# Linear attention and a hard-swish MLP on one core: the leftover tokens' x turned by a crossbar DMA, and w_in's first pieces gated earlier

## The chip, the core and the metric

The kernel runs on one core of a Trainium2 chip. The core has a TensorE for matmuls (PE in the profile, PEld for its weight loads), a VectorE (DVE), a ScalarE (ACT), a GpSimd (POOL) and a SyncE (SP). DMAs are issued by SP, ACT or POOL, each in the order of its own instruction stream, and move data through the core's 16 DMA engines. The metric is the device time of one execution in microseconds; lower is better. The kernel before took 325.93 us (median of three runs, 325.25 to 325.99).

## What is computed

```python
def _attn_ref(q, k, v, omega):               # q, k, v: (8 batches, 8 heads, 576 tokens, 64), f32
    q_s, k_s = q * scale, k * scale          # scale = 64 ** -0.25
    def phi(x):                              # omega: (128 features, 64)
        h = einsum('bhsd,md->bhsm', x, omega) - sum(x * x, -1) / 2
        return exp(h - max(h, -1)) / sqrt(m)
    q_p, k_p = phi(q_s), phi(k_s)
    kv = einsum('bhsm,bhsd->bhmd', k_p, v)
    z = sum(k_p, axis=2)
    num = einsum('bhsm,bhmd->bhsd', q_p, kv)
    den = einsum('bhsm,bhm->bhs', q_p, z)[..., None] + 1e-06
    return num / den

def _moe_ref(x, w_in, w_out):                # x: (4608, 512), w_in: (512, 2048), w_out: (2048, 512)
    h = x @ w_in
    return (h * clip(h + 3, 0, 6) / 6) @ w_out
```

x is the attention's result with the heads of one token side by side. Each batch has 576 tokens: 512 that the kernel calls main, and 64 leftovers.

## The kernel before

**Blocks.** The MLP runs in nine blocks of 512 tokens. Blocks 0 to 7 are the main tokens of batches 0 to 7; block 8 collects the leftovers of all eight batches. Of each block, mm1 (L826; in two halves of 256 tokens for block 0, L854) multiplies x by w_in in 16 steps of four matmuls each, ACT and DVE form the activation gT, and mm2 (L885) multiplies gT by w_out in 4 chunks of 128 tokens. A chunk has four quarters of four matmuls; quarter g needs piece g of w_out. The result goes through osb (four buffers, filled by ACT or DVE) and an out DMA that SP issues.

**Attention of one batch** (L538). k and q are turned so that the head dimension lies on the partitions: kT and qT. The PE does this for batches 0 and 1 (the groups Tk and Tq, L422); from batch 2 on SP issues crossbar transposes (Tdmak and Tdmaq, L622). K (L632) multiplies kT by omega, ACT takes the exponential, and DVE reduces a maximum per row, whose reciprocal scales the rows of v (vc, L737, on POOL or DVE). Q (L649) does the same for q without the maximum. For each of four pairs of heads m, kv (L750, L752) sums over the tokens, num (L773) multiplies by the queries' features, in two parts A and B, and div (L789, DVE) divides and writes x in token order into xb. A pair's part B holds the last main group (i = 3) and the leftovers (i = 4).

**x for the MLP.** xb has two buffers, for even and odd batches: 128 partitions by 4 pairs by 640 columns, that is five groups of 128 per pair, the fifth one being the leftovers. The main groups are turned into xT, by the PE for batches 0 and 1 (X), by one crossbar transpose per pair from batch 2 on (Xdma, L818). The leftovers are turned into xS, for every batch, by e_S (L684): four 64-column matmuls against the identity matrix, here called S.0 to S.7, and a copy from PSUM by DVE or ACT (Sev). mm1 of block 8 reads xS.

**Weights and loads.** w_in comes in four pieces and w_out in four (L467, L474), and from batch 1 on also k and q: POOL issues these DMAs, because they cast f32 to bf16. v and the first batch go over SP. Each load has a gate: a key in the list of reads, whose writer must have finished. `W_GATE` (L335) names the gates of the four w_in pieces: v's landing. Batch 1's k waits for w_in's piece 2 and its q for piece 3 (L927), w_out for the landing of batch 1's q (L928), batch 2's k and q for w_out's pieces 2 and 3.

**What sets the order.** Every operation is recorded by `op` with the engines that may do it, its cost, its priority and its dependencies. A planner (`schedule`, L103) then runs a model of all engines and DMA queues and fixes which engine does what and in which order; each engine gets one stream in that order, with semaphore waits where a dependency crosses engines. For a DMA the model uses `occ`, the time in its queue, and `lat`, the time from there until the data may be used. Changing a number in the model can therefore change the order of every engine from that point on, and adds or removes no computation. In the first 20 us the planner fills the PE's gaps with matmuls of a constant tile (L459, idle).

In POOL's stream of before, the beginning after the identity matrix is: two casts of k, four casts of q, w_in piece 0 (wi0), vc of pair 0 (vc.0.0), wi1, wi2, wi3, vc.0.2, vc.0.3, then batch 1's k and q, and the four pieces of w_out.

Of the kernel before, what the change touches and what calls it, by code (L numbers as in the profile page):

```python
# [41 lines left out]
class Prog:  # L42
# [60 lines left out]
    def schedule(self):  # L103
# [68 lines left out]
        while len(order) < n:  # L172
# [45 lines left out]
            if o.group is not None:  # L218
                free[e] = st + o.issue
                flow(free[e], True)  # L220
                queues.setdefault(e, []).append([o, occ, free[e]])
                flow(1e9, False)
            else:
                free[e] = st + occ
                o.end = free[e]
# [89 lines left out]
def _emit(nc, es, q, k, v, omega, w_in, w_out, out):  # L315
# [19 lines left out]
    W_GATE = [("v32", 0, 1), ("v32", 0, 3), ("v32", 1, 3), ("v32", 1, 3)]  # L335
# [37 lines left out]
    xb = [sbt("xb%d" % u, [128, NJ, 640], BF16) for u in range(2)]  # L373
# [54 lines left out]
    op("SP", 0.2, lambda E: E.dma_start(om32[:], omega), -9.8, writes=["om32"], group="dom", inc=16, lat=1.8,  # L428
# [38 lines left out]
    def w_in_piece(i, gate):  # L467
        f0, f1 = WI[i]
        op("POOL", 0.72 * (f1 - f0), lambda E: E.dma_start(  # L469
            wi[:, :, 128 * f0:128 * f1], w_in[:, 128 * f0:128 * f1].rearrange("(c p) f -> p c f", p=128)),  # L470
           -8.6 + 0.05 * i, reads=gate, writes=[("wi", i)], group="dwi%d" % i, inc=16, lat=2.0, name="wi%d" % i,
           issue=0.85, packet=91.0)

    def w_out_piece(g, gate):  # L474
        op("POOL", 2.95, lambda E: E.dma_start(
            wo[:, 4 * g:4 * g + 4, :], w_out[512 * g:512 * g + 512, :].rearrange("(c p) e -> p c e", p=128)),
           -0.2 + 0.05 * g, reads=gate, writes=[("wo", g)], group="dwo%d" % g, inc=16, lat=2.0, name="wo%d" % g,
# [6 lines left out]
    def load(b, eng, gates):  # L484
# [4 lines left out]
        def dma(part, dst, src, n, keys, gate, prio, run):  # L489
# [4 lines left out]
               group="d" + part + ("c" if cast else "") + (str(pb) if b and part != "v" else ""), inc=16, lat=1.9,  # L494
# [43 lines left out]
    def attention(b):  # L538
# [80 lines left out]
        else:  # L619
            for t, cst, dst in (("k", KB[pb], kT), ("q", QB[pb], qT)):  # L620
                for i, (x0, x1) in enumerate(((0, 10), (10, 18))):
# [4 lines left out]
                       lat=1.9, name="Tdma%s.%d.%d" % (t, b, i), issue=1.2, packet=24.0)  # L626
# [55 lines left out]
        vxs = Virt(ring)  # L682

        def e_S(E):  # L684
            for j in range(NJ):
                ins = E.matmul(ring.t[vxs.slot][:, 64 * j:64 * j + 64], xb[pb][:, j, 512:640], ident[:, 0:64],
                               start=True, stop=True)
            return ins

        op("PE", 4 * 0.03, e_S, pos(11) if b else LATE, reads=[("xb", pb, j, 2) for j in range(NJ)] + ["ident"], writes=[vxs],  # L690
           alloc=[vxs], lat=0.25, slack=sl, spare=sp, name="S.%d" % b)
        op(EV_T, both(256), evac(lambda: xS[:, :, 64 * b:64 * b + 64],
                                 lambda: ring.t[vxs.slot][:, 0:256].rearrange("p (j t) -> p j t", j=NJ)),
           pos(11) if b else LATE, reads=[vxs], writes=[("xS", b)], name="Sev.%d" % b)

    def leftover(m0, m1):
# [8 lines left out]
        def e_num(E):  # L705
# [15 lines left out]
            xb[0][:, m0:m1, 512:640].rearrange("p m (a d) -> p m a d", a=2), psum()[:, :, :, 0:64],  # L721
# [3 lines left out]
    def pair(b, m, t):  # L725
# [33 lines left out]
        xv = xb[pb][:, m, :].rearrange("p (i a d) -> p a i d", a=2, d=D)  # L759

        def tail(part, i0, i1):
# [27 lines left out]
            op("DVE", dvet(128 * n), lambda E: E.tensor_tensor(xv[:, :, i0:i1, :], psum()[:, :, :, 0:64], rbc, ALU.mult),  # L789
               t + 0.01, reads=[vn, ("rec", ru)], writes=[("xb", pb, m, x) for x in part + [2] * (i1 == 5)], name="div" + nm + pt)  # L790

        def turn_x(i0, i1, part):
# [4 lines left out]
            def e_x(E):  # L797
                for i in range(i0, i1):
                    ins = turn(E, vx, b, i - i0, xb[pb][:, m, 128 * i:128 * i + 128])
# [17 lines left out]
        else:  # L817
            op("SP", 0.9, lambda E: E.dma_start_transpose(  # L818
                xT[pb][:, m, :].rearrange("p (t k) -> p t k", t=4), xb[pb][:, m, 0:512]),
               t + 0.03, reads=[("xb", pb, m, x) for x in range(2)], writes=[("xT", pb, m, x) for x in range(2)],  # L820
               group="dxT%d_%d" % (pb, m), inc=16, lat=1.9, name="Xdma" + nm, issue=1.2, packet=24.0)
# [63 lines left out]
    def mm2(blk, tc):  # L885
# [5 lines left out]
        for ci, (c0, c1) in enumerate(cols):  # L891
# [22 lines left out]
            for p0, np_, dst in dsts:  # L914
# [3 lines left out]
                   writes=[("out", blk, tc, p0, ci)], group="dout%d_%d%s" % (ou, p0, "b" if ci else ""), inc=16, lat=2.0,  # L918
                   name="out.%d.%d" % (blk, tc), packet=84.0)

    for b in range(B):
# [4 lines left out]
        elif b == 1:  # L926
            load(1, (), {"k": [("wi", 2)], "q": [("wi", 3)], "v": [("kb", 1, 16)]})  # L927
            for g, key in enumerate((("qb", 1, 16),("qb", 1, 16),("qb", 1, 16),("qb", 1, 16))):  # L928
# [68 lines left out]
```

## Time and profile before

The profile is one execution, taken by the hardware profiler.

| | |
|---|---|
| median of three runs | 325.93 us (325.25 to 325.99) |
| the profiled execution | 325.8 us, of which the span of its instructions is 324.0 us |
| PE busy | 316.0 us (98% of the span) |
| DVE, ACT, POOL busy | 209.8, 190.8, 77.9 us |
| granted TensorE clock | 0.999 of full speed |
| first matmul of mm1 | 20.37 us after the span's start |
| S groups on the PE (L686) | 32 matmuls, 33.3 to 251.7 us |
| crossbar transposes of xT (L818) | 24, from 83.1 to 249.5 us |

A line of a timeline has the start and the length in us, the engine, the source line, the operation with the tile that it writes and those that it reads, its shape, and how many such instructions follow each other; in brackets is the idle time before it and what ended that. SPq is SP's DMA issue. A line of the waits has the engine and line that waited, for whom, and the sum, the count and the longest of the waits. Matmuls are pipelined, so that one's length is more than its spacing to the next. The DMA share is the mean busy share of the 16 DMA engines; it counts overlapping transfers and can exceed 1.

### The profile page before, as it was taken

Reading aid. Unit: us, or ns where it says so; the run is one execution under the profiler, and the core shown is the slowest. Engines: PE = TensorE matmul, PEld = TensorE weight load, DVE = VectorE, ACT = ScalarE, POOL = GpSimd, SP = SyncE. Lnnn points to the kernel's source line nnn. Section 1 sums busy time; section 2 is a strip of 40 time slices with the busy share of each in tenths; the row PEclk is TensorE's granted clock in tenths of the full one; section 3 lists DMA queues with packets and bytes.
Section 4 is the critical chain, followed back from the end, with each engine's and each line's share of the span. In section 5 each row is a group of like instructions: output and inputs, shape, how many; then the busy total and the mean of one; then the engine's idle time right before and its main releaser. Section 6 shows DMA issues by size and latency. Waiting matters only on the chain.

```text
span 324.0 us, 5860 instructions
## 1 busy us (share of the span) xinstructions
PE 316.0 (98%) x2224; PEld 174.9 (54%) x2260; DVE 209.8 (65%) x464; ACT 190.8 (59%) x388; POOL 77.9 (24%) x107
## 2 busy tenths in 40 slices
PE   8999989999999999999999999999999999999996
PEld 6779755455654545555455545555555444444443
DVE  4988876498877828865776577756865354433411
ACT  3977963499585518865776477647674353444400
POOL 2825624055252402620154022402010000000000
PEclk9999999999999999999999999999999999999999
DMA  8999999999932997999479863996012201000024
GB/s 249 253 193 157 226 182 187 292 139 188 250 85 51 171 177 203 126 198 142 170 105 155 182 195 48 170 205 212 14 53 58 74 6 58 33 34 32 32 67 97
DMA packets 89516, 44.33 MB, mean 137 GB/s; under 512 B 56080, under 2 KB 85008, under 8 KB 89488
## 3 DMA queue, kind: packets, MB, share of 16 engines
q1 hardware_dynamic: 62272, 30.85, 40.1%
q0 software_dynamic: 26512, 12.46, 31.6%
q10 hardware_dynamic: 704, 0.66, 0.7%
q8 instruction: 18, 0.29, 0.4%
q14 instruction: 10, 0.08, 0.1%
HBM read 36.73 MB, written 9.44 MB: 143 GB/s over the span
## 4 chain that ended last, share of the span: by engine, by line
PE 85%; DMA 9%; POOL 2%; issue 1%; SPq 1%; DVE 0%
PE p L899 38%; PE p L841 34%; PE p L632 4%; PE p L649 4%; DMA wi<-in_moe_w_in_dram 3%; DMA wo<-in_moe_w_out_dram 3%; PE p L773 3%; DMA k<-in_q_dram 2%; PE p L750 2%; DMA q<-in_q_dram 2%; POOL k L493 1%; SPq L493 1%; PE p L752 0%; POOL wi L469 0%; POOL qb L411 0%
## 5 line engine op out<-in xcount | busy, mean ns | idle before, releaser
L899 PE MATMUL p<-wo,gT 128*128 128x512 bf16 (+2 forms) x571 | 139.7, 373 | 2.4 <-DMA wo<-in_moe_w_out_dram 1.3
L849 DVE SCALAR_TENSOR_TENSOR gT<-tsb,p 128x512 bf16<-128x512 bf16 x128 | 87.2, 684 | 58.0 <-ACT tsb L847 57.4
L847 ACT ACTIVATE tsb<-p 128x512 bf16<-128x512 f32 x128 | 77.1, 603 | 72.0 <-PE p L841 71.9
L841 PE MATMUL p<-xT,wi 128*128 128x512 bf16 x439 | 107.3, 379 | 0.5
L899 PEld LDWEIGHTS p<-wo,gT 128*128 128x128 bf16 x592 | 55.8, 98 | 56.8 <-ACT qpT L653 1.2
L841 PEld LDWEIGHTS p<-xT,wi 128*128 128x128 bf16 x448 | 42.9, 98 | 46.0 <-ACT qpT L653 0.2
L641 DVE TENSOR_REDUCE mx<-kp 128x4 f32<-128x512 bf16 x72 | 47.4, 674 | 15.9 <-ACT kp L638 15.9
L638 ACT ACTIVATE kp<-p 128x512 bf16<-128x512 f32 x72 | 41.5, 621 | 14.6 <-PE p L632 14.6
L653 ACT ACTIVATE qpT<-p 128x512 bf16<-128x512 f32 (+1 forms) x80 | 42.4, 576 | 3.4 <-PE p L649 3.3
L737 POOL TENSOR_TENSOR vc<-v,cc 128x512 bf16<-128x512 f32 x24 | 25.2, 1048 | 43.6 <-DVE cc L733 27.8
L789 DVE TENSOR_TENSOR xb<-p,rec 128x384 bf16<-128x384 f32 (+1 forms) x64 | 28.6, 476 | 0.0
L632 PE MATMUL p<-om,kT 128*128 128x256 bf16 x144 | 24.3, 273 | 0.0
L649 PE MATMUL p<-qT,om 128*128 128x512 bf16 (+1 forms) x76 | 23.2, 357 | 0.1
L410 ACT COPY osb<-p 128x512 f32<-128x512 f32 x25 | 14.8, 592 | 9.7 <-PE p L899 9.6
L411 DVE COPY osb<-p 128x512 f32<-128x512 f32 (+2 forms) x12 | 7.8, 646 | 18.2 <-PE p L899 18.1
L672 POOL TENSOR_TENSOR vcl<-vl,cc 64x260 bf16<-64x260 f32 x9 | 5.6, 622 | 54.3 <-DVE cc L668 30.9
L773 PEld LDWEIGHTS p<-kvz,qpT 128*128 128x128 bf16 x312 | 14.2, 98 | 7.3 <-DVE kvz L411 0.4
L632 PEld LDWEIGHTS p<-om,kT 128*128 128x128 bf16 x144 | 13.2, 98 | 9.0
L841 PE MATMUL p<-xS,wi 128*128 128x512 bf16 x62 | 16.2, 379 | 0.1
L493 POOL DMA_DIRECT2D k<-in_k_dram x12 | 9.2, 777 | 28.3 <-PE p L632 14.1
L866 PE MATMUL p<-xT,wi 128*128 128x256 bf16 x128 | 15.9, 273 | 0.0
L773 PE MATMUL p<-kvz,qpT 128*128 128x65 bf16 x312 | 15.6, 194 | 0.0
(70 smaller groups left out, 225.4 us busy)
## 6 DMA issues: line engine op xcount, KB each, us to landing
out_dram<-osb SPq DMA_DIRECT2D x32, 256.0 KB, 3.1
v<-in_v_dram SPq DMA_DIRECT2D x14, 512.0 KB, 5.6
wi<-in_moe_w_in_dram POOLq DMA_DIRECT2D x4, 512.0 KB, 8.1
k<-in_k_dram POOLq DMA_DIRECT2D x8, 256.0 KB, 4.6
k<-in_q_dram POOLq DMA_DIRECT2D x8, 256.0 KB, 5.7
wo<-in_moe_w_out_dram POOLq DMA_DIRECT2D x4, 512.0 KB, 9.9
kb<-in_k_dram POOLq DMA_DIRECT2D x6, 256.0 KB, 4.6
qb<-in_q_dram POOLq DMA_DIRECT2D x6, 256.0 KB, 5.7
```

Of the source, the lines that this page charges most:

```text
L632: ins = E.matmul(ring.t[vK.slot][:, 256 * i:256 * i + 256], kT[:, 2 * u + i, :], om[:].rearrange("d t m -> d (t m)"), start=True, stop=True)
L638: op("ACT", actt(512), lambda E, u=u, vK=vK: E.activation(kp[pb][:, 4 * u:4 * u + 4, :].rearrange("p c m -> p (c m)"), ring.t[vK.slot], AF ...
L641: op("DVE", dvet(512), lambda E, u=u: E.reduce_max(mx[pb][:, 4 * u:4 * u + 4], kp[pb][:, 4 * u:4 * u + 4, :], axis=AX.X), pos(u) + 0.03, r ...
L649: op("PE", mmt(n), lambda E, vQ=vQ, lh=lh: E.matmul(ring.t[vQ.slot][:, 0:n], om[:, lh, :], src, start=True, stop=True), p + 0.045 * lh, re ...
L653: op("ACT", actt(n), lambda E, vQ=vQ, lh=lh: E.activation(dst(lh), ring.t[vQ.slot][:, 0:n].rearrange("m (j t) -> m j t", t=128), AF.Exp, s ...
L737: op(EV_V if b else V0, {"POOL": 1.2, "DVE": dvet(512)}, lambda E: E.tensor_tensor(vcm[:, :, 0:D], v32[:, m, :, :], cbc, ALU.mult), t, rea ...
L773: ins = E.matmul(d[:, hh, i - i0, :], qpT[pb][:, o:o + 128], kvz[m][:, 65 * hh:65 * hh + 65], start=True, stop=True)
L789: op("DVE", dvet(128 * n), lambda E: E.tensor_tensor(xv[:, :, i0:i1, :], psum()[:, :, :, 0:64], rbc, ALU.mult), t + 0.01, reads=[vn, ("rec ...
L841: ins = E.matmul(ring.t[vh.slot], wi[:, c, 128 * f:128 * f + 128], xv[:, c, :], start=(c == 0), stop=(c == NJ - 1))
L847: op("ACT", actt(512), lambda E: E.activation(tsb[tu][:], ring.t[vh.slot], AF.Relu, bias=0.5, scale=1.0 / 6.0), t - 0.1, reads=[vh], write ...
L849: op("DVE", dvet(512), lambda E: E.scalar_tensor_tensor(gT[gu][:, f, :], tsb[tu][:], 1.0, ring.t[vh.slot], ALU.min, ALU.mult), t - 0.1, re ...
L899: ins = E.matmul(ring.t[vo.slot][:, 0:c1 - c0], gT[gu][:, f, 128 * tc:128 * tc + 128], wo[:, f, c0:c1], start=(f == 0), stop=(f == NF - 1))
```

## The change

- xb stays as large, but its columns are laid out anew: first the four pairs' main groups (512 columns each), then the four pairs' leftovers (128 each) as one contiguous part. `xm` and `xl` are views of the two parts. div of part B writes its two groups with one access pattern whose step reaches from the main part to the leftover part.
- For batch 0, S stays on the PE. For batches 1 to 7 the four matmuls and their copy are replaced by Sdma: SP issues one crossbar transpose of 64 partitions by 512 columns of xb into xS.
- `W_GATE`: w_in's pieces 0 and 1 are gated on the landing of v's leftover rows (vl) instead of v's main rows; pieces 2 and 3 as before on v11, the last of v's main rows.
- The planner's model of a DMA: its transfer starts 0.9 us (1.25 on POOL) after the issue, and `lat` is about 0.9 to 1.0 us shorter (1.0 instead of 1.9 or 2.0).

In the streams that the planner makes of this: POOL has three casts of q, wi0, wi1, vc.0.0, wi2, wi3, the fourth cast of q, vc.0.2. SP issues out.0.0 (block 0, chunk 0) ahead of batch 2's main v instead of behind it, and has Sdma.1 between out.0.2 and the transposes of batch 2's q; the later Sdma stand behind the last Xdma of their batch. On the PE, w_out's first quarters are mm2.0.0 and mm2.0.1, then kv.1.0 and the second quarter of mm2.0.0; before, a Q and kv.1.1 stood ahead of that second quarter too. mm2.0.3 is finished ahead of block 1. Later on K, Q, kv and num stand at other places among the quarters of mm2.

```diff
@@ schedule
-                queues.setdefault(e, []).append([o, occ, free[e]])
+                queues.setdefault(e, []).append([o, occ, free[e] + (1.25 if e == "POOL" else 0.9)])
@@ _emit
-    W_GATE = [("v32", 0, 1), ("v32", 0, 3), ("v32", 1, 3), ("v32", 1, 3)]
+    W_GATE = [("vl", 0)]*2+[("v32", 1, 3)]*2
...
-    xb = [sbt("xb%d" % u, [128, NJ, 640], BF16) for u in range(2)]
+    XW = NJ * 640
+    xb = [sbt("xb%d" % u, [128, XW], BF16) for u in range(2)]
+    xm = [t[:, 0:NJ * 512].rearrange("p (j c) -> p j c", c=512) for t in xb]
+    xl = [t[:, NJ * 512:XW].rearrange("p (j c) -> p j c", c=128) for t in xb]
...
@@ w_in_piece (w_out_piece and the out DMA likewise)
-           -8.6 + 0.05 * i, reads=gate, writes=[("wi", i)], group="dwi%d" % i, inc=16, lat=2.0, name="wi%d" % i,
+           -8.6 + 0.05 * i, reads=gate, writes=[("wi", i)], group="dwi%d" % i, inc=16, lat=1.0, name="wi%d" % i,
@@ load, Tdma, Xdma, omega: lat=1.9 (1.8) becomes lat=1.0 (0.9)
@@ attention
-        vxs = Virt(ring)
-
-        def e_S(E):
-            for j in range(NJ):
-                ins = E.matmul(ring.t[vxs.slot][:, 64 * j:64 * j + 64], xb[pb][:, j, 512:640], ident[:, 0:64],
-                               start=True, stop=True)
-            return ins
-
-        op("PE", 4 * 0.03, e_S, pos(11) if b else LATE, reads=[("xb", pb, j, 2) for j in range(NJ)] + ["ident"], writes=[vxs],
-           alloc=[vxs], lat=0.25, slack=sl, spare=sp, name="S.%d" % b)
-        op(EV_T, both(256), evac(lambda: xS[:, :, 64 * b:64 * b + 64],
-                                 lambda: ring.t[vxs.slot][:, 0:256].rearrange("p (j t) -> p j t", j=NJ)),
-           pos(11) if b else LATE, reads=[vxs], writes=[("xS", b)], name="Sev.%d" % b)
+        if b < 1:
...
+        else:
+            op("SP", 0.6, lambda E: E.dma_start_transpose(
+                xS[:, :, 64 * b:64 * b + 64], xb[pb][0:64, NJ * 512:XW]),
+               pos(12), reads=[("xb", pb, j, 2) for j in range(NJ)], writes=[("xS", b)], group="dxS", inc=16, lat=1.0,
+               name="Sdma.%d" % b, issue=1.2, packet=24.0)
@@ pair
-        xv = xb[pb][:, m, :].rearrange("p (i a d) -> p a i d", a=2, d=D)
+
+        def xv(i0, i1):
+
+            far = NJ * 512 + 128 * m
+            step = far - (512 * m + 384) if i1 == 5 else 128
+            return bass.AP(xb[pb], 512 * m + 128 * i0, [[XW, 128], [64, 2], [step, i1 - i0], [1, 64]])
...
-            op("DVE", dvet(128 * n), lambda E: E.tensor_tensor(xv[:, :, i0:i1, :], psum()[:, :, :, 0:64], rbc, ALU.mult),
+            op("DVE", dvet(128 * n), lambda E: E.tensor_tensor(xv(i0, i1), psum()[:, :, :, 0:64], rbc, ALU.mult),
...
-                xT[pb][:, m, :].rearrange("p (t k) -> p t k", t=4), xb[pb][:, m, 0:512]),
+                xT[pb][:, m, :].rearrange("p (t k) -> p t k", t=4), xm[pb][:, m, :]),
```

Where the old text reads xb's columns of a pair, the new one reads xm; where it reads columns 512 to 640 of a pair, xl. The list of w_out's gates is written in another way and holds the same.

## The prediction

> **What bounds the kernel now.** I read the engine totals first, then the table by stage, because a share over the whole span mixes stages.
>
> ```profile
> PE 316.0 (98%) x2224; PEld 174.9 (54%) x2260; DVE 209.8 (65%) x464; ACT 190.8 (59%) x388; POOL 77.9 (24%) x107
> ...
> 20.00:36.00 16.00, 15.88 (x184) 14.55 (x185) 13.35 (x34) 12.83 (x28) 6.71 (x10) 1.00 1.25 207
> 36.00:48.00 12.00, 10.59 (x102) 7.11 (x102) 10.09 (x23) 9.32 (x21) 4.89 (x8) 1.00 1.14 178
> 60.00:97.00 37.00, 36.74 (x279) 20.65 (x283) 30.43 (x71) 29.02 (x65) 15.40 (x19) 1.00 1.03 181
> ```
>
> After the stretch, its length and the PE's busy time come the other engines, the clock, the DMA share and GB/s. The PE is idle for 0.1 to 0.3 us in each stage from 20 us on, except in 36 to 48, where 1.41 us are missing. That a busy PE is not waiting inside shows in the spacing: four 512-column matmuls start every 0.86 us, in the chain from 48 to 306 us, whoever runs beside them. So from mm1's first matmul (20.37 us) to the last (321 us) an instruction taken off the PE is worth its spacing, and one hole is left. The waits and the PE's timeline show the hole:
>
> ```profile
> PE p L899 <- DMA wo<-in_moe_w_out_dram: 1.3, 2, 0.9
> ...
> 41.00 1.02 PE L899 MATMUL p<-wo,gT 128*128 128x512 bf16 x4 [0.92 <-DMA wo<-in_moe_w_out_dram]
> ...
> 43.04 0.38 PE L649 MATMUL p<-qT,om 128*128 128x512 bf16 x1
> 43.25 0.42 PE L750 MATMUL p<-vc,kp 128*128 128x65 bf16 x8
> ...
> 44.12 1.04 PE L899 MATMUL p<-wo,gT 128*128 128x512 bf16 x3 [0.39 <-DMA wo<-in_moe_w_out_dram]
> ```
>
> The first mm2 waits for w_out's piece 0 (until 41.00), and its second quarter for piece 1 (until 44.12). What puts these so late is the chain of work that ended last:
>
> ```profile
> 14.12 9.04 DMA wi<-in_moe_w_in_dram
> 23.44 2.30 POOL k L493 x3
> 26.69 7.34 DMA k<-in_q_dram
> 35.06 9.02 DMA wo<-in_moe_w_out_dram
> ```
>
> w_in's piece 2 lands at 23.2 and lets POOL issue batch 1's k (23.44), q follows, and q's landing (34.03) lets POOL issue w_out (34.32). Every link is a gate written in the code, so an earlier w_in moves all of it. Where w_in begins is POOL's doing:
>
> ```profile
> 9.88 1.29 POOL L411 CAST qb<-q 128x512 bf16<-128x512 f32 x2 [0.27 <-POOL qb L411]
> 11.36 0.94 POOL L469 DMA_DIRECT2D wi<-in_moe_w_in_dram  x1 [0.19 <-issue]
> 12.32 1.06 POOL L737 TENSOR_TENSOR vc<-v,cc 128x512 bf16<-128x512 f32 x1
> 13.31 2.30 POOL L469 DMA_DIRECT2D wi<-in_moe_w_in_dram  x3
> 15.60 2.25 POOL L737 TENSOR_TENSOR vc<-v,cc 128x512 bf16<-128x512 f32 x2
> ```
>
> Piece 0 follows four casts of q; the 0.19 us before it is issue, no wait.
>
> **Part 1: seven S groups leave the PE.** In the timeline S.1 starts at 58.77 and the next mm2 at 58.88: 0.11 us; S.2 takes 0.12 (90.13 to 90.25). Batches 1 to 7 lose theirs: 7 x 0.11 = 0.77 us, all after 44 us on a full PE. The seven copies to xS (0.42 us on DVE, 0.38 on ACT) go too, beside the PE: worth 0.
>
> **Part 2: seven Sdma come to SP.** The nearest row is the transpose of xT (L818): 1.19 to 2.22 us of SP each, landing after 2.4 to 7.0, median 3.5; an Sdma moves half as much. I take 1.2 and 3.5. The reader of xS is block 8's mm1 (first at 279.3 us; S.7 ran at 251.6), the next writer of that xb is two batches on, some 35 us; so neither waits. In the changed order of SP each Sdma stands behind the last Xdma of its batch, or later (for batch 1, whose x the PE turns, behind out.0.2), so its data are there, and it holds up only what follows it: an out, a transpose of q or the next v. Cover: SP waits 64.6 us in all for osb copies. Bounds: 0, and the stall in rival C.
>
> **Part 3: the layout.** The second div of a pair writes two pieces a far step apart instead of 128: same elements, same instruction (0.48 us mean, L789). DVE sits idle 58 us before g (L849) for ACT. 0, and if each of its 28 cost 0.1 more, still 0 at the end. The transposes' source rows of 512 elements stay whole.
>
> **Part 4: w_in earlier.** POOL's new order is three q casts, wi0, wi1, vc.0.0, wi2, wi3, the fourth cast, vc.0.2. wi0 waits for vl, which lands at 4.83 + 5.5 = 10.3; the third cast ends at 9.88 + 0.645 = 10.53. So wi0 is issued 0.65 us earlier (one cast), near 10.7. Whether data follow: the DMA moves 318 to 350 GB/s until 12.5, 28 in 13.0 to 13.5, 68 in 13.5 to 14.0, then 190. A POOL load reaches its rate some 2.6 us after its issue (11.36 to 14.0; 23.44 to 26), so the new flow starts near 13.3, in an empty stretch. I take the whole 0.65; bounds 0 (it only takes v's turn) and 1.0 (the dip to 148 GB/s at 16 to 17 closes too, as wi1 now stands behind wi0 at once). The Trainium skill, page "DMA: Bandwidth & Descriptors", section "Issuing engines are not separate DMA queues", speaks against it: whatever engine issues them, the transfers share the 16 DMA engines and interleave. If that were all, w_in would only push v later, 0 of the 0.65 would remain and the sum below would be -0.25; the empty microsecond in the trace is why I stay with 0.65.
>
> POOL works without a gap from 9.88 to 17.85 and has the same instructions before vc.0.2, so vc.0.2 moves only if a gate is late: wi2 waits for v11, which lands at 7.05 + 6.3 = 13.35, just as POOL gets there. 0 to 0.7 us; kv.0.2 follows at once (16.74), and mm1 would start that much later. Cover: the hole at w_out. The fourth cast now ends near 15.6, its turn on the PE near 15.8, and its copy on ACT came at 16.4 anyway.
>
> **Part 5: the planner's new DMA times change the order.** (a) Before the second quarter of mm2.0.0 stood one Q and kv.1.1 more; now they come after it. They filled the hole from 43.04 to 43.56: 0.52 us of work goes behind the wait. (b) The last quarter of mm2.0.3 comes before block 1 instead of inside it: same work. (c) SP issues out.0.0 ahead of batch 2's v; rival C. (d) The rest are swaps of K, Q, kv and num among mm2 quarters. Between the last num of batches 2, 4, 5 and 6 and the block that needs its Xdma still lie 8 to 10 quarters (7 to 9 us), against 1.2 + 3.5 us for issue and landing. 0.
>
> **Sum.** The second quarter starts when piece 1 lands: 44.12 - 0.65 = 43.47. The PE, free for mm2 at 40.03 before (its last Q began at 39.81 and took 0.22), needs two quarters and kv.1.0 (0.86 + 0.86 + 0.31) to get there: 42.1. So up to 1.4 us of a late start is covered by the wait that remains. Behind it comes the old work, plus 0.52, minus 0.77: -0.65 + 0.52 - 0.77 = -0.90 us. The profiled execution took 325.8 us (span 324.0); 324.9 follows, and 325.93 - 0.90 = 325.0 for the median, which lies 0.13 above that execution. 0.3% is 0.98 us, about what a measurement of this kernel can tell from no change: my value lies just inside.
>
> **Rivals.**
> A, w_in gains nothing (0 to 0.4 us): the flow only takes v's place. For it: vl, v and ql are still moving at 12.5. Against: the empty stretch. -0.25 - (0 to 0.4): 325.3 to 325.7.
> B, more is won: 1.0 us from w_in gives -1.25, 324.7. For it: the dip. Against: w_out's flow has the same dip (156 and 151 GB/s at 39 to 41 us) with its pieces queued at once.
> C, slower: SP brings batch 2's q transposes too late.
>
> ```profile
> 52.60 8.32 SPq L622 DMA_TRANSPOSE kT<-kb x2
> 60.97 1.05 SPq L916 DMA_DIRECT2D out_dram<-osb  x2
> 62.12 4.20 SPq L622 DMA_TRANSPOSE qT<-qb  x2
> ```
>
> The two kT transposes held SP 3.8 and 4.5 us behind v's megabyte. Now v goes out some 1.2 us later (behind out.0.0), and Sdma.1 stands before qT. The first qT landed at 62.1 + 5.2 = 67.3 and was wanted at 70.13. Late by 1.2 + 1.2 it lands at 69.7; wanted, after the new order, near 70.13 - 0.65 + 0.52 + 0.86 - 0.33 = 70.5 (a quarter of mm2.0.3 more before it, K2.7 and S.1 less). If Sdma.1 costs 4.5 as a kT did, it lands at 73.0, 2.5 us late: +1.6, 327.5. It decides above 1.9 us late (+1.0), so from 72.4 on. The page "Advanced Engine Details and Errata", section "X-Bar Transpose (TRN2)", has transposes as fast as regular DMAs, which by itself would make C's price 0; the stretch 64 to 65 us, with transposes in flight, shows a DMA share of 3.10 at 131 GB/s, so here they take more.
> D, v11 comes so late that the start slips by more than the 1.4 us covered: with 2.0 us, -0.3, 325.6. Against: at most 0.7 was seen as possible.
>
> **Chances.** The forecast (w_in 0.45 to 0.85 earlier, no new stall: 324.8 to 325.2) 0.44; its value lies 0.08 us inside the bound, so I count 0.18 of it as faster and 0.26 as within 0.3%. B 0.16, faster. A and D together 0.14, within. C 0.16: 0.13 slower by over 0.3%, 0.03 within. A plan remade in this many places can stall where I found no reason: 0.10, slower. Faster 0.18 + 0.16 = 0.34, same 0.26 + 0.14 + 0.03 = 0.43, slower 0.13 + 0.10 = 0.23. The range, 324.4 to 326.8, reaches past B and into the middle of C; the forecast's own is 324.8 to 325.2.
>
> **What would show it.** Right: no S matmuls after batch 0; POOL's wi0 near 10.7; k of batch 1 issued near 22.8; mm2's second quarter near 43.5 with a wait of about 1 us before it, the first with little; the stretches after 48 us full. Wrong: k still issued at 23.4 (A); a wait of Q or K for qT or kT in 62 to 73 us (C); mm1 starting after 21.5 (D); a wait of block 2 to 7's mm1 for xT.

## The result, and the profile after

The changed kernel took 324.59 us (median of six runs, 324.03 to 325.16); the kernel before took 325.59 us in six runs. The ratio is 0.9971, with a 95% interval from 0.9953 to 0.999. In a later session, with 12 and 35 runs, it was 324.22 us against 325.56 us, ratio 0.9961 (0.9939 to 0.9982). The gain is therefore 1.0 to 1.3 us, and the forecast was 0.9. Ratios and intervals leave out a run that is more than 1.5% above the fastest of its kernel (one of old_model, two of wo_early), while medians and ranges count every run. The profiled execution of the changed kernel took 324.03 us with a span of 322.2 us, 1.8 us below that of before. In the code of after the lines are: mm1 L855 (first block L880), mm2 L913, X and the turns by PE L425, K L635, Q L652, kv L759 and L761, w_in L472, w_out L478, vc L746, Sdma L700, crossbar transposes of k and q L625.

First the engine totals of the page, and the same three stages as before (stretch, length, busy PE, PEld, DVE, ACT and POOL, clock, DMA share, GB/s):

```profile
PE 315.0 (98%) x2198; PEld 174.3 (54%) x2233; DVE 207.3 (64%) x458; ACT 189.1 (59%) x387; POOL 77.7 (24%) x107
...
20.00:36.00 16.00, 15.84 (x185) 14.23 (x183) 13.53 (x34) 12.69 (x27) 8.05 (x12) 1.00 1.22 204
36.00:48.00 12.00, 11.89 (x112) 8.15 (x113) 9.42 (x22) 10.51 (x27) 5.00 (x7) 1.00 1.10 170
60.00:97.00 37.00, 36.74 (x267) 20.44 (x271) 30.99 (x70) 29.01 (x64) 12.56 (x17) 1.00 1.03 186
```

The one stage with missing time, 36 to 48 us, now lacks 0.11 us of PE work instead of 1.41, and the 0.11 is no wait (see the account below). All of the PE's waits for other engines (who waited for whom; sum, count, longest in us):

```profile
PE p L462 <- DVE fill L457: 1.3, 1, 1.3
PE p L425 <- POOL qb L414: 0.6, 2, 0.5
PE p L425 <- DVE xb L803: 0.2, 1, 0.2
```

These three lie ahead of mm1 or at its beginning. The PE's timeline at the place of the old hole:

```profile
40.49 0.27 PE L652 MATMUL p<-qT,om 128*128 128x256 bf16 x1
40.60 1.89 PE L913 MATMUL p<-wo,gT 128*128 128x512 bf16 x8
42.32 0.42 PE L759 MATMUL p<-vc,kp 128*128 128x65 bf16 x8
42.58 0.22 PE L761 MATMUL p<-vcl,kp 128*128 128x130 bf16 x1
42.64 1.03 PE L913 MATMUL p<-wo,gT 128*128 128x512 bf16 x4
```

No wait for w_out is left, at the first quarter or at the second. The second quarter needs w_out's piece 1. It was issued at 33.71 us and landed 8.9 us later, at 42.6; before, it was issued at 35.06 and took 9.0 us (first line after, second line before; the last number is the time to landing):

```profile
wo<-in_moe_w_out_dram POOLq DMA_DIRECT2D x1, 512.0 KB, 8.9
wo<-in_moe_w_out_dram POOLq DMA_DIRECT2D x1, 512.0 KB, 9.0
```

The PE came to the quarter at 42.64, just as the piece landed. The chain that ended last, which ran through w_out's load at 35.06 us before, has no load of w_out in it now. What put w_out forward is POOL's stream:

```profile
9.96 0.61 POOL L414 CAST qb<-q 128x512 bf16<-128x512 f32 x1 [0.34 <-DMA q<-in_q_dram]
10.70 1.69 POOL L472 DMA_DIRECT2D wi<-in_moe_w_in_dram  x2
12.40 1.06 POOL L746 TENSOR_TENSOR vc<-v,cc 128x512 bf16<-128x512 f32 x1
14.06 1.55 POOL L472 DMA_DIRECT2D wi<-in_moe_w_in_dram  x2 [0.60 <-DMA v<-in_v_dram]
15.60 0.63 POOL L414 CAST qb<-q 128x512 bf16<-128x512 f32 x1
16.32 2.22 POOL L746 TENSOR_TENSOR vc<-v,cc 128x512 bf16<-128x512 f32 x2
22.76 2.29 POOL L496 DMA_DIRECT2D k<-in_k_dram  x3 [4.23 <-DMA wi<-in_moe_w_in_dram]
25.24 2.73 POOL L496 DMA_DIRECT2D k<-in_q_dram  x4 [0.18 <-issue]
32.96 2.99 POOL L478 DMA_DIRECT2D wo<-in_moe_w_out_dram  x4 [5.00 <-DMA k<-in_q_dram]
```

w_in starts at 10.70 instead of 11.36, batch 1's k at 22.76 instead of 23.44, w_out at 32.96 instead of 34.32. The price stands in the fourth line: w_in's piece 2 waits 0.60 us for v11, and everything on POOL behind it moves. So does the first matmul of mm1:

```profile
21.05 0.82 PE L880 MATMUL p<-xT,wi 128*128 128x256 bf16 x6
```

It started at 20.37 before. SP's stream, where rival C would have shown:

```profile
51.57 1.10 SPq L496 DMA_DIRECT2D v<-in_v_dram  x2
52.77 7.45 SPq L625 DMA_TRANSPOSE kT<-kb  x2
60.26 1.05 SPq L930 DMA_DIRECT2D out_dram<-osb  x2
61.36 1.18 SPq L700 DMA_TRANSPOSE xS<-xb  x1
62.64 1.25 SPq L625 DMA_TRANSPOSE qT<-qb  x1
```

The kT transposes take long, as before, but they are over before the new transpose, which takes 1.18 us.

**An account of the PE.** A simple sum orders all the runs below. From mm1's first matmul to the PE's last, the span is work plus holes. A hole is the time between two groups beyond the spacing of the first one; the table has those of 0.05 us or more. The Q ahead of the first mm2 of before is this one:

```profile
39.81 0.27 PE L649 MATMUL p<-qT,om 128*128 128x256 bf16 x1
```

It takes 0.11 us, as the one at 40.49 above does, which mm2 follows at 40.60. So the holes of before go from 39.92 to 41.00 and from 43.56 to 44.12 and make 1.64. The bracketed waits are a little shorter than the holes, because the profile sets the end of a matmul later than its spacing. Some profiles lack the records of a few matmuls (before has 2224 matmuls for 2260 weight loads, after 2198 for 2233); a gap of one spacing (0.22 us for 512 columns) where such a record is missing is no hole. Work is the end, minus the start, minus the holes.

| profile | mm1 starts | holes: where | PE ends | work |
|---|---|---|---|---|
| before | 20.37 | 1.64: w_out | 320.97 | 298.96 |
| gates_only | 21.69 | none seen | 320.64 | 298.95 |
| s_on_pe | 20.85 | 0.70: w_out | 320.53 | 298.98 |
| wo_early | 20.53 | 0.89: w_out; 0.73: block 1's xT | 321.12 | 298.97 |
| after | 21.05 | none seen | 319.20 | 298.15 |
| after_again | 21.75 | none seen | 319.90 | 298.15 |
| fill_hole | 20.50 | 0.07: w_out | 318.72 | 298.15 |
| k_early | 20.55 | 0.84: block 1's xT | 319.59 | 298.20 |
| old_model | 21.62 | 0.62: vc at 160 us | 320.46 | 298.22 |
| old_gates | 20.60 | 0.84: block 1's xT; 0.22: two small ones | 319.88 | 298.22 |
| cast_in_gap | 20.43 | 0.44: w_out; 0.24: mm1 at 39 us | 319.30 | 298.19 |
| wi3_late | 21.42 | 0.50: w_out; 0.74: vc at 160 us | 320.84 | 298.18 |
| both_late | 20.66 | 0.41: w_out; 1.88: vc at 46 us; 1.06: block 1's xT; 0.16: at 31 us | 322.33 | 298.16 |
| pe_pad | 20.95 | 0.47: w_out | 322.85 | 301.43 |

So the 1.77 us by which the PE ends earlier in the profile pair are 0.81 of work and 1.64 of holes, less 0.68 for the later start. The work falls into three groups: 298.95 to 298.98 with S on the PE, 298.15 to 298.22 without seven of its groups, and 301.43 with the 28 groups of pe_pad added. The steps are 0.8 us for seven groups and 3.28 for 28, about 0.117 us for each.

### The profile page after: what moved, and what is told of

It reads as the page before. It is cut to its first block, busy times and chain, and to the rows that moved or that the text cites. A ratio compares the mean times of both kernels' runs of the same rounds, so it can differ in the third digit from the quotient of the medians.

```text
span 322.2 us, 5822 instructions
## 1 busy us (share of the span) xinstructions
PE 315.0 (98%) x2198; PEld 174.3 (54%) x2233; DVE 207.3 (64%) x458; ACT 189.1 (59%) x387; POOL 77.7 (24%) x107
## 4 chain that ended last, share of the span: by engine, by line
PE 88%; ACT 4%; DVE 1%; issue 1%
PE p L913 38%; PE p L855 32%; PE p L652 4%; PE p L880 4%; PE p L635 3%; PE p L787 3%; ACT kp L641 2%; PE p L759 2%; PE p L425 1%; ACT tsb L861 1%; PE p L761 0%; ACT qT L413 0%; DVE xb L803 0%; DVE gT L863 0%; ACT tsb L889 0%
## 5 line engine op out<-in xcount | busy, mean ns | idle before, releaser
L913 PE MATMUL p<-wo,gT 128*128 128x512 bf16 (+2 forms) x578 | 139.5, 373 | 0.8
L855 PE MATMUL p<-xT,wi 128*128 128x512 bf16 x434 | 106.4, 379 | 0.7
L913 PEld LDWEIGHTS p<-wo,gT 128*128 128x128 bf16 x592 | 56.2, 98 | 57.4
L855 PEld LDWEIGHTS p<-xT,wi 128*128 128x128 bf16 x448 | 42.6, 98 | 45.1 <-ACT qpT L656 0.2
L641 ACT ACTIVATE kp<-p 128x512 bf16<-128x512 f32 x72 | 40.5, 616 | 18.6 <-PE p L635 18.5
L656 ACT ACTIVATE qpT<-p 128x512 bf16<-128x512 f32 (+1 forms) x80 | 41.7, 576 | 3.5 <-PE p L652 3.5
L746 POOL TENSOR_TENSOR vc<-v,cc 128x512 bf16<-128x512 f32 x24 | 25.5, 1064 | 35.8 <-DVE cc L742 26.8
L635 PE MATMUL p<-om,kT 128*128 128x256 bf16 x144 | 23.1, 273 | 0.0
L652 PE MATMUL p<-qT,om 128*128 128x512 bf16 (+1 forms) x74 | 21.6, 356 | 0.2
L414 DVE COPY osb<-p 128x512 f32<-128x512 f32 (+2 forms) x12 | 7.7, 646 | 20.7 <-PE p L913 20.7
L635 PEld LDWEIGHTS p<-om,kT 128*128 128x128 bf16 x144 | 13.6, 98 | 8.9
L855 PE MATMUL p<-xS,wi 128*128 128x512 bf16 x63 | 16.2, 379 | 0.1
L880 PE MATMUL p<-xT,wi 128*128 128x256 bf16 x128 | 15.9, 273 | 0.0
L759 PEld LDWEIGHTS p<-vc,kp 128*128 128x128 bf16 x256 | 11.8, 98 | 6.1 <-POOL vc L746 0.3
```

The source lines that it names most:

```text
L635: ins = E.matmul(ring.t[vK.slot][:, 256 * i:256 * i + 256], kT[:, 2 * u + i, :], om[:].rearrange("d t m -> d (t m)"), start=True, stop=True)
L641: op("ACT", actt(512), lambda E, u=u, vK=vK: E.activation(kp[pb][:, 4 * u:4 * u + 4, :].rearrange("p c m -> p (c m)"), ring.t[vK.slot], AF ...
L652: op("PE", mmt(n), lambda E, vQ=vQ, lh=lh: E.matmul(ring.t[vQ.slot][:, 0:n], om[:, lh, :], src, start=True, stop=True), p + 0.045 * lh, re ...
L656: op("ACT", actt(n), lambda E, vQ=vQ, lh=lh: E.activation(dst(lh), ring.t[vQ.slot][:, 0:n].rearrange("m (j t) -> m j t", t=128), AF.Exp, s ...
L855: ins = E.matmul(ring.t[vh.slot], wi[:, c, 128 * f:128 * f + 128], xv[:, c, :], start=(c == 0), stop=(c == NJ - 1))
L880: ins = E.matmul(ring.t[vh.slot][:, 256 * g:256 * g + 256], wi[:, c, 128 * (f + g):128 * (f + g) + 128], xT[0][:, c, 256 * half:256 * half ...
```

## The experiments

Each kernel was timed against the kernel before in its own session (medians of before: 325.27, 325.36 and 325.56 us in three sessions).

### The gates alone

```diff
-    W_GATE = [("v32", 0, 1), ("v32", 0, 3), ("v32", 1, 3), ("v32", 1, 3)]
+    W_GATE = [("vl", 0)]*2+[("v32", 1, 3)]*2
```

in the kernel before; all else, S included, stays.

> The kernel before with only the four gates of w_in changed (v's leftover rows for pieces 0 and 1, v11 for 2 and 3); S stays on the PE, the planner's DMA model stays. Theory (the changed kernel's time is the start of mm1, plus PE work, plus the hole before w_out's piece 1): POOL issues w_in near 10.7 and w_out near 33.0, mm1 starts near 21.05 (0.68 later, because wi2 waits for v11 and the fourth cast and vc.0.2 stand behind it), and the PE's hole of 0.97 + 0.56 us at mm2's first two quarters closes: span 324.0 + 0.68 - 1.5 = 323.2, 0.8 us under before. Rival (the gates only move v back, nothing is won before w_out): hole stays, span 324.0 to 324.7.

325.05 us (324.53 to 325.90) against 325.27, ratio 0.9994 (0.9974 to 1.0014). No difference can be claimed. The hole is gone from the profile, and the start is late (21.69). Part of that is chance: the first cast of q on POOL began at 9.39 us, against 8.32 in the profile of before. The expected 0.8 us under before lies inside the interval and isn't shown. What did change is the spread: in the same session the runs of before reached from 324.13 to 327.48.

### S back on the PE

```diff
-        if b < 1:
+        if b < B:
```

in the changed kernel, so that the old S and its copy serve all eight batches; the gates, the layout and the planner's numbers stay new.

> The changed kernel with S and its copy on the PE for all eight batches, no Sdma; new xb layout, gates and planner model stay. Theory: seven S groups of 0.11 us come back on a full PE: 0.77 us over the changed kernel (span 322.2 to 323.3 there), still 0.2 to 0.8 us under before. Rival (the crossbar transposes cost on SP and the DMA queues what they save on the PE): within 0.2 us of the changed kernel, or faster.

325.07 us, ratio 0.9995 (0.9975 to 1.0016). The changed kernel stands at 0.9971 and 0.9961 against the same base, 0.24% to 0.34% lower, which is 0.8 to 1.1 us. The PE shows the price of S directly: from block 1's first matmul to its end it is busy for 260.36 us here and for 259.66 us in both profiles of the changed kernel. The six groups S.2 to S.7 lie in that stretch, so one costs 0.117 us, and seven cost 0.82. The rival, that SP and the DMA queues lose what the PE saves, fell with this. The wait at the second quarter is back, because the start was 0.20 us earlier than in after's profile and w_out was issued 0.66 us later (33.62):

```profile
43.15 1.04 PE L913 MATMUL p<-wo,gT 128*128 128x512 bf16 x4 [0.54 <-DMA wo<-in_moe_w_out_dram]
```

### More of the same on the PE

```diff
@@ kv, batches 1 to 7, each of the four pairs
+            for _ in range(4 * PAD if b else 0):
+                E.matmul(o[:, 0:64], ident[:], ident[:, 0:64], start=True, stop=True)
```

with PAD = 1 in the changed kernel: 28 groups of four 64-column matmuls, each as long as an S, are added; kv starts its sums anew after them.

> The changed kernel with four extra 64-column matmuls ahead of each kv of batches 1 to 7 (28 groups, each the size of an S group, into the bank that kv clears next; the plan is the same). Theory: each group is worth its spacing of 0.11 us on a full PE: 28 x 0.11 = 3.1 us over the changed kernel, some 2 us over before. Rival (the PE has slack inside its busy time): under 1.5 us over the changed kernel.

327.33 us (six runs), ratio 1.0078 (1.0054 to 1.0101), 2.7 us above the first median of the changed kernel. The stretch from block 1's start to the end grew from 259.66 to 262.46 us; 24 of the 28 groups lie in it, which makes 0.117 us each. A short group on the full PE costs what its spacing says, at seven groups and at 28.

### The planner's old numbers

```diff
-                queues.setdefault(e, []).append([o, occ, free[e] + (1.25 if e == "POOL" else 0.9)])
+                queues.setdefault(e, []).append([o, occ, free[e]])
@@ every DMA
-  lat=1.0
+  lat=1.9
```

(2.0 for w_in and w_out, 1.8 for omega, as before), with everything else of the change kept.

> The changed kernel with the planner's old DMA numbers (lat 1.9 or 2.0, no delay after the issue); Sdma, layout and gates stay. One Q and kv.1.1 then stand ahead of mm2.0.0's second quarter again, as in the kernel before. Theory: the planner's numbers move work round a hole that is closed anyway, so the time is that of the changed kernel within 0.3 us, with no wait of the PE for w_out. Rival (the new model is what made it faster, by better order all along the kernel): the gain of 1 us goes, stalls of 0.1 to 0.5 us appear in the stages after 60 us.

324.87 us, ratio 0.9993 (0.9974 to 1.0011); one of its twelve runs took 332.75 us, the others 323.92 to 325.41. No wait for w_out, but the plan made from these numbers lets kv wait for POOL's vc in batch 4:

```profile
160.32 0.43 PE L759 MATMUL p<-vc,kp 128*128 128x65 bf16 x8 [0.46 <-POOL vc L746]
```

The hole is 0.62 us and the work 298.22, that of the other kernels without S. So the new numbers are not what closes the hole at w_out. The stall is about what the kernel lost against the changed one, but that the plan made it isn't shown: vc waits for batch 4's v, and wi3_late (below) waits at the same place with the changed kernel's order.

### The fourth cast into the wait for v11

```diff
+    names = [o.name for o in G.order]
+    cast4 = G.order.pop(names.index("castq0.1B"))
+    G.order.insert([o.name for o in G.order].index("wi2"), cast4)
```

after the planner has run, in the changed kernel. POOL then does the cast in the 0.60 us in which it waited.

> The changed kernel, its plan kept, with one move in POOL's order: the fourth cast of q goes ahead of wi2, into the time in which POOL waits for v11. Theory: vc.0.2 and mm1 start 0.3 to 0.6 us earlier than in the changed kernel (near 20.5 instead of 21.05), w_in and w_out are issued as before the move; but the PE then waits that much for w_out's piece 1, so the time stays within 0.3 us of the changed kernel. Rival (the start is what sets the end now that the hole is closed): 0.4 to 0.6 us under the changed kernel, no wait for w_out.

324.51 us against 325.36, ratio 0.9966 (0.9946 to 0.9986), and mm1 starts at 20.43, 0.62 earlier than in after's profile. POOL's stream, and the PE at the second quarter:

```profile
13.35 0.70 POOL L414 CAST qb<-q 128x512 bf16<-128x512 f32 x1
14.00 1.55 POOL L472 DMA_DIRECT2D wi<-in_moe_w_in_dram  x2
15.55 1.06 POOL L746 TENSOR_TENSOR vc<-v,cc 128x512 bf16<-128x512 f32 x1
```

```profile
42.21 0.22 PE L761 MATMUL p<-vcl,kp 128*128 128x130 bf16 x1
42.71 1.04 PE L913 MATMUL p<-wo,gT 128*128 128x512 bf16 x4 [0.28 <-DMA wo<-in_moe_w_out_dram]
```

The start that was won came back as a wait: the PE arrives earlier, w_out does not (its piece 1 landed at 42.7, in after at 42.6). That is what "the late start is covered by the wait" meant, seen from the other side.

### Also w_in's last piece behind vc.0.3

```diff
+    move("castq0.1B", "wi2")
+    move("wi3", "k00.1")
```

> As the run with the cast in the gap, and w_in's piece 3 is issued behind vc.0.2 and vc.0.3 instead of ahead of them. Theory: mm1 starts 0.9 us earlier than in the changed kernel (near 20.1), piece 3 still lands in time for its matmuls (its flow follows piece 2's), batch 1's k and q are issued as before, and the PE's wait for w_out grows to about 0.5 to 1 us: within 0.3 us of the changed kernel. Rival (start sets the end): 0.9 us under it.

324.48 us, ratio 0.9976 (0.9955 to 0.9998): no better than the cast alone. The piece that was put off is a gate, and batch 1's q waits for it:

```profile
27.05 2.73 POOL L496 DMA_DIRECT2D k<-in_q_dram  x4 [1.35 <-DMA wi<-in_moe_w_in_dram]
```

Nor did the start come earlier. mm1 began at 21.42, 0.99 later than in cast_in_gap, and POOL's first cast of q 0.98 later (9.14 against 8.16): the first loads were late, and the move itself won nothing. vc.0.2, no longer behind wi3, waited for DVE's cc instead:

```profile
16.54 1.04 POOL L746 TENSOR_TENSOR vc<-v,cc 128x512 bf16<-128x512 f32 x1 [0.75 <-DVE cc L742]
```

The profiled execution took 325.77 us, nearly the longest of the twelve (323.63 to 325.81). It has two waits that after doesn't have, though the order there is the same:

```profile
159.69 0.43 PE L759 MATMUL p<-vc,kp 128*128 128x65 bf16 x8 [0.22 <-DVE vc L746]
160.59 0.43 PE L759 MATMUL p<-vc,kp 128*128 128x65 bf16 x8 [0.19 <-POOL vc L746]
```

SP's two kT transposes at 137 us took 6.17 us here and 4.84 in after, and batch 4's v, which vc needs, was issued at 152.56 instead of 150.67. The edit changes nothing at that place, so the two waits, 0.74 us of holes together, most likely belong to this execution.

### w_out gated earlier, in the kernel before

```diff
-            for g, key in enumerate((("qb", 1, 16),("qb", 1, 16),("qb", 1, 16),("qb", 1, 16))):
+            for g, key in enumerate((("kb", 1, 16),) * 4):
```

> The kernel before with one key changed: w_out is gated on the landing of batch 1's k instead of its q. POOL then issues it right behind q's loads, near 29 instead of 34.3. Theory: w_out lands in time, the PE's 1.5 us of waits before mm2's first two quarters go, and the time falls by 1.2 to 1.5 us against before. Rival (the hole covers something else that is late, or w_out's flow delays v or q of batch 1 by as much): under 0.5 us, with new waits for q, v or vc between 30 and 60 us.

327.35 us, ratio 1.0043 (1.0007 to 1.0079): slower. POOL issued w_out at 29.34 us, 5 us earlier, but a piece now took 13.7 us (median) to land instead of 9.9:

```profile
DMA to landing us min/median/max: 10.2/13.7/16.4
```

```profile
42.91 1.04 PE L899 MATMUL p<-wo,gT 128*128 128x512 bf16 x4 [0.72 <-DMA wo<-in_moe_w_out_dram]
...
60.76 1.47 PE L841 MATMUL p<-xT,wi 128*128 128x512 bf16 x6 [0.56 <-ACT xT L410]
```

Five microseconds at the issue bought about one at the second quarter of mm2, and the plan made with it waits for xT at block 1. The theory that an earlier w_out shortens the time fell here. What makes the median longer isn't in the profile: its execution took 325.96 us, among the shorter of 324.97 to 330.66, and its holes add up to 1.62 us, as before's do. The Trainium skill, page "DMA: Bandwidth & Descriptors", section "Issuing engines are not separate DMA queues", says that all DMAs of a core end up on the same 16 engines and interleave there. The landings agree: w_out, issued by POOL, took 13.7 us instead of 9.9, and batch 1's two big loads of v, issued by SP at the same time, took 9.4 us (median) instead of 7.8.

### The same gate in the changed kernel, with both POOL moves

```diff
-            for g, key in enumerate((("qb", 1, 16),)*4):
+            for g, key in enumerate((("kb", 1, 16),)*4):
...
+    move("castq0.1B", "wi2")
+    move("wi3", "k00.1")
```

> The changed kernel with the two moves on POOL (fourth cast ahead of wi2, wi3 behind vc.0.3) and w_out gated on batch 1's k. Theory (start and hole are the two terms left beside the PE's work): start 0.9 us earlier and no wait for w_out: 0.9 us or more under the changed kernel, near 323.5. Rival (batch 1's q or v come late instead, because w_out shares the DMA engines with them): no faster than the changed kernel, with waits of Q or kv of batch 1.

325.69 us, ratio 1.0007 (0.9984 to 1.0029): all of the gain is lost. The wait for w_out is down to 0.25 us, and kv waits instead, for a vc that waits for v:

```profile
43.99 1.55 POOL L746 TENSOR_TENSOR vc<-v,cc 128x512 bf16<-128x512 f32 x1 [4.36 <-DMA v<-in_v_dram]
...
45.69 0.42 PE L759 MATMUL p<-vc,kp 128*128 128x65 bf16 x8 [1.72 <-POOL vc L746]
```

That is what the rival said: v comes late beside w_out. Block 1's mm1 waits too, 0.89 us for xT, which no theory had.

### The changed kernel once more

> The changed kernel once more, in one session with the next three, so that they are compared with it and not only with the kernel before. Theory (the change is worth about 1 us, all of it the S groups and a shorter wait at the start): 0.8 to 1.2 us below the kernel before. Rival (the first difference was the luck of a few runs): less than 0.4 us below.

324.22 us (12 runs, 323.66 to 324.93) against 325.56, ratio 0.9961 (0.9939 to 0.9982). The result repeats. The start in this profile is 0.70 us later than in the first (21.75; the first cast of q at 9.46 instead of 8.34), and with no hole to absorb it the PE also ends 0.70 later (319.90).

### The old gates in the changed kernel

```diff
-    W_GATE = [("vl", 0)]*2+[("v32", 1, 3)]*2
+    W_GATE = [("v32", 0, 1), ("v32", 0, 3), ("v32", 1, 3), ("v32", 1, 3)]
```

> The changed kernel with the old gates of w_in, so the crossbar transposes alone. The planner, run anew, puts two Q groups, K.1.5, kv.1.0 and a turn of q around the second quarter of the first mm2, so the wait for w_out should now lie at its first quarter, some 1.5 to 2 us at 39 to 42 us. Theory (seven S groups are worth 0.8 us; the early w_in is worth 0 to 0.5 us): 0.4 to 0.8 us below the kernel before, 0.2 to 0.6 us above the changed kernel. Rival (the gain comes from the early w_in): no more than 0.2 us below the kernel before.

325.72 us (324.88 to 329.36), ratio 1.0021 (0.9987 to 1.0056), 1.5 us above the changed kernel in the same session. By its number the rival won, but its reason isn't shown. The expected wait at w_out's first quarter did not show in the profile: batch 1's q released w_out 6.6 us after its issue (8.4 before), so w_out was issued at 32.73, with the old gates and still earlier than in after. The new plan has another one, which no theory had:

```profile
58.99 0.39 PE L425 MATMUL p<-ident,xb 128*128 128x128 bf16 x4
60.05 2.12 PE L855 MATMUL p<-xT,wi 128*128 128x512 bf16 x9 [0.68 <-ACT xT L413]
```

Block 1's last X group stands directly ahead of its mm1, so its copy on ACT lies open. In after, a quarter of mm2 (0.86 us) stands between:

```profile
58.46 0.39 PE L425 MATMUL p<-ident,xb 128*128 128x128 bf16 x4
58.68 1.03 PE L913 MATMUL p<-wo,gT 128*128 128x512 bf16 x4
59.54 2.75 PE L855 MATMUL p<-xT,wi 128*128 128x512 bf16 x12
```

With the holes taken off, the work is 298.22: S is gone here as well, and its gain is spent at this place. That stall is about half of the 1.5 us; the rest is open. The profiled execution was the shortest of the twelve (324.88), and it doesn't show what made others take up to 329.36.

### The hole filled

```diff
+    move(names.index("castq0.1B"), "wi2")
+    names = [x.name for x in G.order]
+    quarters = [i for i, n in enumerate(names) if n == "mm2.0.0"]
+    move(quarters[1], "K1.6")
```

in the changed kernel: the early cast, and Q.1.2 and kv.1.1 ahead of the second quarter of mm2.0.0, as they stood in the kernel before.

> The changed kernel with two edits to the written-out order: the fourth cast of q goes ahead of w_in's piece 2 on POOL (which brought mm1 0.6 us earlier and a wait of 0.28 us for w_out back), and on the PE the second quarter of the first mm2 goes behind Q.1.2 and kv.1.1, 0.52 us of work that needs no w_out. Theory (a start 0.6 us earlier is lost only because the wait for w_out takes it back): with the wait filled, 0.3 to 0.6 us below the changed kernel. Rival (the end is set elsewhere, or the moved Q only makes another instruction wait): within 0.2 us of the changed kernel.

324.01 us (323.52 to 325.14), ratio 0.9959 (0.9937 to 0.9982). The profile does what the theory says: mm1 starts at 20.50 and all but nothing waits for w_out (0.07 us).

```profile
42.30 0.42 PE L759 MATMUL p<-vc,kp 128*128 128x65 bf16 x8
42.56 0.22 PE L761 MATMUL p<-vcl,kp 128*128 128x130 bf16 x1
42.69 1.04 PE L913 MATMUL p<-wo,gT 128*128 128x512 bf16 x4
```

Its profiled execution took 323.65 us, the shortest of all profiles. But the median is only 0.21 us below the changed kernel, less than either's runs scatter. It can't be told from it, and no version here is shown to beat the change.

### Batch 1's k and q gated one piece earlier

```diff
-            load(1, (), {"k": [("wi", 2)], "q": [("wi", 3)], "v": [("kb", 1, 16)]})
+            load(1, (), {"k": [("wi", 1)], "q": [("wi", 2)], "v": [("kb", 1, 16)]})
```

and the fourth cast ahead of w_in's piece 2, in the changed kernel.

> The changed kernel with the fourth cast of q ahead of w_in's piece 2, and with batch 1's k gated on w_in's piece 1 instead of 2 and its q on piece 2 instead of 3: each link of the chain k, q, w_out is issued about one piece (1 to 1.5 us) earlier, into the stretch from 23 to 25.5 us where the DMA moves little. Theory (the chain of gates sets w_out, and the DMA has room): w_out's issue 1 us or more earlier, no wait for w_out, mm1 still at about 20.4, so 0.3 to 0.6 us below the changed kernel. Rival (k and q only take the place of w_in's last pieces, as w_out did with k's place when it was put forward): the first k groups wait for w_in's pieces 2 and 3 near 24 to 28 us, and the time is the changed kernel's or up to 1 us more.

324.60 us (324.22 to 326.44), ratio 0.9978 (0.9953 to 1.0004), 0.4 us above the changed kernel. The theory missed; the rival had the time right and its reason wrong. POOL's stream:

```profile
20.18 2.29 POOL L496 DMA_DIRECT2D k<-in_k_dram  x3 [2.15 <-DMA wi<-in_moe_w_in_dram]
22.70 2.73 POOL L496 DMA_DIRECT2D k<-in_q_dram  x4 [0.23 <-DMA wi<-in_moe_w_in_dram]
31.98 2.99 POOL L478 DMA_DIRECT2D wo<-in_moe_w_out_dram  x4 [6.55 <-DMA k<-in_q_dram]
```

k and q go out 2.4 us earlier than with the later gates (fill_hole: 22.62 and 25.11), q takes 9.3 us until it releases w_out instead of 8.05, and 1.2 us remain at w_out (31.98 against 33.16). The DMA had room, and no k group waited for w_in's last pieces. But the plan has the bare X group of old_gates again:

```profile
59.92 1.25 PE L855 MATMUL p<-xT,wi 128*128 128x512 bf16 x5 [0.68 <-ACT xT L413]
```

## Why the prediction was right, and where it wasn't

The time was right: 0.9 us less was forecast, 1.0 and 1.3 us less were measured. The median of 324.59 us lies 0.4 below the 325.0 of the forecast, mostly because the kernel before took 325.59 in these six runs and not 325.93. For the chances it is the border between "within 0.3%" and "faster": the two ratios are 0.29% and 0.39% below 1.

- **What bounds the kernel.** Right that the PE is full, but the 0.1 to 0.3 us that the prediction reads as idle in every stage are matmuls without a record. after_again, which lacks none (2233 matmuls, 2233 weight loads), is busy 37.00 of 37.00 us from 60 to 97.
- **Part 1, S.** Right: 0.11 us each was forecast, 0.117 measured with six groups and again with 24; the work of the profile pair differs by 0.81.
- **Part 2, Sdma on SP.** Right: worth nothing at the end. The issue took 1.18 us (1.2 forecast). The landing took 5.1 us (median) instead of the 3.5 I took from xT's transposes, though half as much is moved; nobody waits for it.
- **Part 3, the layout.** Right: div takes 476 ns, as before.
- **Part 4, w_in earlier.** Right about the cause: wi0 at 10.70 and k at 22.76, where 10.7 and 22.8 were forecast. The empty microsecond of the DMA is filled (13.0 to 13.5 us: 147 GB/s instead of 28; 13.5 to 14.0: 197 instead of 68). That is against rival A. In the profile w_out's issue moved by 1.36 us instead of 0.65, since q's landing took 7.7 us instead of 8.4 from issue to release. Kernels with the new gates had 6.8, 7.3, 8.2 and 8.7 in other profiles and old_gates 6.6, so this part is the run's and not the change's.
- **v11 as a gate.** The wait on POOL was 0.60 us and the start slipped by 0.68, the upper end of the 0 to 0.7 named.
- **Part 5a and the sum, the step that was mis-sized: w_out's landing.** The forecast has the second quarter start at 44.12 - 0.65 = 43.47, behind "a wait of about 1 us". In both profiles of the changed kernel it waits for nothing. The PE's side of the sum was right: it was to get there at 42.1 (41.95, with the last Q ahead of mm2 at 0.11 us and not 0.22), plus the slip of 0.68 that is 42.63, and it got there at 42.64. But piece 1 landed at 42.6 instead of some 43.4: it was issued 0.70 us earlier than forecast (35.06 to 33.71 is 1.35 and not 0.65), and it was 0.1 us quicker. The quarter came 0.83 earlier than forecast, and what lies behind it ended 0.29 earlier relative to it, against 0.25 forecast (0.52 less 0.77). The sum then reads -0.65 - 0.83 - 0.29 = -1.77, and the PE's end moved by 1.77. So the causes and their order were right, and one term was mis-sized by the luck of single profiles: from mm1's start to the landing of piece 1 it is 21.5 us in both profiles of the changed kernel, 20.7 in gates_only, 21.2 in old_model, 22.1 in pe_pad and 22.2 in s_on_pe, and the changed kernel's PE needs 21.6 for its way. The cover is used up there: the same wait can be 0 in one execution and over half a microsecond in the next. That the medians, over 6 and 12 runs, moved by 1.0 and 1.3, so near to the 0.9, is in part luck too.
- **Part 5c, rival C.** Wrong, as counted on: Sdma.1 took 1.18 us, qT followed at 62.64, where the issue took 1.25, and the first Q of batch 2 ran at 69.70 without a wait.
- **Part 5d, swaps at no cost.** Right for this plan: no wait after 48 us. It was not a safe assumption. Four of the kernels planned anew wait at block 1's xT, which their edits do not name: 0.56 us (wo_early), 0.68 (old_gates and k_early) and 0.89 (both_late). The 0.46 us at vc in old_model may be the execution's, as in wi3_late. The 0.10 that I had kept for such a stall was less than it deserved.

Where does the gain come from? S is worth 0.8 us, shown by s_on_pe, by pe_pad and by the account of the PE. The rest, 0.2 to 0.5 us, would be the gates' and the plan's, but no run shows it apart: the kernels that keep S and have the new gates are 0.22 (gates_only) and 0.20 us (s_on_pe) under before, each within its interval. The gates do move batch 1's k: it is issued 15.1 to 15.2 us behind POOL's first cast of q with the old gates (before, wo_early, old_gates) and 14.0 to 14.5 with the new ones (k_early, which has gates of its own for k, aside). But w_out comes behind q, and q takes between 6.6 and 8.7 us to release it (9.3 in k_early); old_gates has no hole at w_out either. So whether the hole is there depends on the execution as much as on the gates.

Single executions scatter, and not equally. In one session before ran from 324.06 to 327.66, old_gates from 324.88 to 329.36 and after_again from 323.66 to 324.93; in another, gates_only from 324.53 to 325.90 beside 324.13 to 327.48 for before. The shortest runs of before and after_again are 0.4 us apart, the medians 1.3. It looks as if the kernels with vl as the gate of w_in's first pieces had fewer long executions, but that isn't shown: both_late, with vl, ran from 324.63 to 327.48, and old_model has the run of 332.75. Which wait makes the long ones long is open. No kernel with the old gates has a profile of a long execution; the one of wi3_late, with vl, points to late first loads and to a v held up on SP.

## What to carry to other kernels

On an engine that is full from one point to the end, an instruction is worth its spacing, and a late start is worth nothing only as long as a later wait still covers it: work out what is left of the cover after every other step has moved too. An account of start, holes and work prices an instruction to some 0.1 us from single profiles, where whole executions scatter by one or more; it has to allow for missing records. A cast or a transfer that moves past a gate brings the gate's own landing onto the queue, so ask what lands last before it and what stands behind it. When a planner makes the order anew, compare its streams at every place where a copy was covered by a neighbour, because a stall of 0.5 to 0.8 us can appear far from the edit and eat the whole gain.

## What I had not expected of the hardware

The first loads of one and the same program land at different times. POOL's first cast of q began between 8.16 and 8.47 us in ten profiles and between 9.14 and 9.46 in four (gates_only, old_model, wi3_late, after_again). The start of mm1 follows, and where no hole is left so does the end: after and after_again differ by 1.12 us at the cast and by 0.70 us at both. With one profile per kernel, a shift of a microsecond at the start belongs to the run before it belongs to the edit.
